# MLP matmuls whose moving columns come from the two halves in turn, with a shorter matmul time in the list scheduler

## Chip, cores and metric

The kernel runs on one core of one Trainium2 chip. The metric is the device time of one execution in microseconds, lower is better.

## What is computed

Random-feature attention over 4 batches, 8 heads, 576 positions (all float32), then two MLPs over its 2304 tokens. The reference, cut:

```python
def _attn_ref(q, k, v, omega):            # (4, 8, 576, 64), omega (128, 64)
    def phi(x):
        h = np.einsum('bhsd,md->bhsm', x, omega) - sum(x * x) / 2
        return np.exp(h - max(h)) / np.sqrt(m)
    q_p, k_p = (phi(q_s), phi(k_s))
    kv = np.einsum('bhsm,bhsd->bhmd', k_p, v)
    return einsum(q_p, kv) / (einsum(q_p, sum(k_p)) + 1e-06)
...
x = attention, as (2304, 512)
h = x @ w_in;  g = h * sigmoid(h);  x = g @ w_out                        # d_ff 2048
g = x @ w_gate;  x = (g * sigmoid(g)) * (x @ w_val) @ w_out2             # d_ff 1536
```

## The kernel before, in words

**Attention** (the first 118 us) works through pairs of heads in steps of 128 positions. Its matmuls (lines 751, 795, 842, and the transposes at 811 and 867) are not touched. Two short bursts of matmuls of a zero tile, 384 columns wide, stand in it: nine at line 734 at the very start, seven at line 903 a little later.

**The MLPs** have four phases in a row: up 1 (`up_phase(0)`, weights `w_in`), down 1 (`down_phase(0)`, `w_out`), up 2 (`w_gate` and `w_val`), down 2 (`w_out2`). The token axis is held in three slices `s` of 2 x 384 columns (`N = 384`, `NSB = 3`), transposed: features on partitions, tokens along the row. Every 2 x 2 block product is done with seven products instead of eight (`PROD`, `ORDER`; operands `A..`/`S..` of the weights, `B..`/`T..` of the activations). Each operand is split into a high part of type float32r and a low part, and a product of two operands is three matmuls: high by high, high by low, low by high. So an up product (`products`, line 1097) is 2 x 3 matmuls, and a down step (line 1472) 2 x 2 x 3; each matmul has 128 x 128 weights and 384 moving columns and adds into one PSUM bank, `ps[b][:, :N]`.

Around the matmuls: ACT copies PSUM banks on (`copy`, lines 1114 and 1413), applies silu (line 1138) and makes high parts (lines 410, 580, 1280, 1331); DVE adds banks (line 1171), makes low parts (lines 423, 591, 1284, 1335) and differences (lines 613, 1355); `conv_job` (lines 322 to 440) loads float64 weights (`L322`), turns them into float32 with ACT (line 343, reads every second word), DVE (lines 350, 357, which reads every second word too) and POOL sums (line 376), and keeps them or stores them to `wd_out` (line 440); line 1123 stores an up phase's result to `g_d`, line 1305 loads it for the down phase.

**The order of the work** on ACT, DVE, POOL and SP is set when the kernel is built, by a list scheduler that runs beside the emission of the matmuls. It keeps a modelled clock per engine (`clk`). After each product, `clk["PE"]` moves on by `6 * MM` (up) or `12 * MM` (down), and `flush` emits all work on the other engines that the model finds ready by then. `MM` is the modelled time of one matmul in us:

```python
    MM = 0.1735
...
            clk["PE"] = t + 6 * MM
...
                    clk["PE"] = t + 12 * MM
```

The engines run their queues in that order, each instruction waiting for what it needs. Nothing on the chip reads `MM`.

Of the kernel before, what the change touches and what calls it, by code (L numbers as in the profile page):

```python
# [42 lines left out]
def kernel(  # L43
# [34 lines left out]
    N = 384  # L78
# [20 lines left out]
    ps = [pp.tile([P, 512], F32, name=f"ps{i}") for i in range(8)]  # L99

    def cut(t, o, n):
        return t[:, o : o + n]

    W_AT, T_AT, X_AT = 0, 7168, 10752
    S_AT, C_AT, R_AT, SUM_AT, XR_AT = 0, 3840, 5376, 7424, 8448
# [126 lines left out]
    def flush(now):  # L232
        while True:
            best = None
            for o in urgent:
                t = o.ready()
                if t is not None and t <= now and (best is None or t < best[0]):
                    best = (t, o)
            if best is None:
                break  # L240
            urgent.remove(best[1])
            best[1].emit()
        while True:

            best = None
            for i, (name, st) in enumerate(streams.items()):
                o = st.best(now + st.ahead, name in ("z", "wd") and clk["dma"] > now + 5.0)
                if o is not None:
                    t = max(o.ready(), clk[o.eng]) + 0.1 * i
                    if best is None or t < best[0]:  # L250
                        best = (t, st, o)
            if best is None:
                break
            best[1].emit(best[2])
# [19 lines left out]
    def need(*keys):  # L274
        for k in keys:
            while k not in T:
                st, o = maker.get(k, (None, None))
                if st is None:
                    u = [o for o in urgent if k in o.outs]
                    if not u:  # L280
                        assert drain(), f"{k} is made nowhere"
                        continue
                    o = u[0]
                need(*o.ins)
                if o.ready() is None:

                    assert drain(), f"{k}: stuck"
                elif k not in T:
                    if st is None:
                        urgent.remove(o)  # L290
                        o.emit()
                    else:
                        while st.q[o.eng][0] is not o:
                            p = st.q[o.eng][0]
                            need(*p.ins)
                            if p.ready() is None:
                                assert drain(), f"{k}: stuck"
                            elif st.q[o.eng][0] is p:
                                st.emit(p)
                        if k not in T and o.ready() is not None:  # L300
                            st.emit(o)

    f_raw = Free("raw", [cut(fa, R_AT + i * 1024, 1024) for i in range(2)])
    f_c = Free("c", [cut(fa, C_AT + i * 512, 512) for i in range(3)])
    f_sum = Free("sum", [cut(fa, SUM_AT, 1024)])
    f_z = Free("z", [])
    f_w = Free("w", [cut(ra, W_AT + i * 1792, 1792) for i in range(6)])
# [748 lines left out]

    later_on.append((1, last_nums))

    MM = 0.1735


    LEND, lent = {(1, 0): ("T3", "T4", "B22",)}, []
# [2 lines left out]
    def up_phase(m, seq, hook):  # L1067
# [17 lines left out]
        def products(n, p, b, start, stop, extra=()):  # L1085
            i, kind, s = seq[n]
            oa, ob = PROD[p]
            need(("W", kind, i), ("X", m, s, ob), *extra)
            wh, wl = (cut(x, OPA[oa] * 256, 256) for x in W[kind, i])
            xh, xl = X[m, s, ob]  # L1090
            t = clk["PE"]
            for k in [("W", kind, i), ("X", m, s, ob), *extra]:
                t = max(t, T[k] + 0.1)
            c = 0
            for j in range(2):
                for l, r in ((wh, xh), (wh, xl), (wl, xh)):
                    nc.tensor.matmul(  # L1097
                        ps[b][:, :N],
                        cut(l, j * P, P),
                        cut(r, j * N, N),  # L1100
                        start=start and c == 0,
                        stop=stop and c == 5,
                        skip_group_check=True,
                    )
                    c += 1
            clk["PE"] = t + 6 * MM
            T[K("P", n, p)] = clk["PE"]
# [79 lines left out]
        for _, n, p in sorted(slots):  # L1187
# [3 lines left out]
            a, b = ps[A[n % 2]], ps[B[n % 2]]  # L1191
            hook(n, p)
            flush(clk["PE"])
            if p == 1:
                products(n, 1, A[n % 2], True, False, [K("h", n - 2, 0)] if n > 1 else [])
                copy(n, 1, b[:, :N], a[:, :N], "AB", free=[("a", n - 2, 3)])
                if m == 0 and n == 0:
                    flush(clk["PE"] + 0.2)
                    later_on.pop(0)[1]()
                    mark(5, 6)  # L1200
            elif p == 6:
                products(n, 6, B[n % 2], False, False, [K("AB", n)])
                copy(n, 6, ps[E][:, :N], b[:, :N], "BE", free=[("a", n - 1, 1)])
            elif p == 5:
# [110 lines left out]
    def down_phase(m, Wd, hook, gap_until=None):  # L1315
# [78 lines left out]
        BANKS = {1: 0, 2: 0, 5: 2, 3: 2, 6: 4, 7: 4, 4: 6}  # L1394
# [55 lines left out]
        for s in range(NSB):  # L1450
            for p in ORDER:
                for k in range(np_):
                    hook(s, p, k)
                    flush(clk["PE"])
                    keys = [K("hi", s, p, k), K("lo", s, p, k)]
                    keys += [("Wd", m, p, g) for g in {2 * k // 3, (2 * k + 1) // 3}]
                    if k == 0 and p in BEFORE:
                        keys += [K("v", s, BEFORE[p], e) for e in range(2)]
                    if k == 0 and p in (1, 5) and s:
                        keys += [K("v", s - 1, {1: "C11", 5: "C12"}[p], e) for e in range(2)]  # L1460
                    need(*keys)
                    t = clk["PE"]
                    for x in keys:
                        t = max(t, T[x] + 0.1)
                    hi, lo = ops.pop((s, p, k))
                    for j in range(2):
                        i = 2 * k + j
                        wh, wl = (cut(t, (i % 3) * 256, 256) for t in Wd[p, i // 3])
                        h, l = cut(hi, j * N, N), cut(lo, j * N, N)
                        for e in range(2):  # L1470
                            for c, (a, b) in enumerate(((wh, h), (wh, l), (wl, h))):
                                nc.tensor.matmul(  # L1472
                                    ps[BANKS[p] + e][:, :N],
                                    cut(a, e * P, P),
                                    b,
                                    start=p in FIRST and i == 0 and c == 0,
                                    stop=p in LAST and i == fp - 1 and c == 2,
                                    skip_group_check=True,
                                )
                    clk["PE"] = t + 12 * MM  # L1480
                    for t in (hi, lo):
                        n = len(lent)
                        lent[:] = [x for x in lent if x is not t]
                        if len(lent) < n:
                            f_op.give(t)
                        elif t is not gap or (s, p) != gap_until and not gone:
                            f_z.give(t)
                        else:
                            gone.append(t)
                    if (s, p, k) == (*(gap_until or (0, 0)), np_ - 1) and not gone:  # L1490
                        f_z.q = deque(x for x in f_z.q if x[0] is not gap)
                        gone.append(gap)
                    if s == NSB - 1 and (k == np_ - 1):
                        for g in range((fp + 2) // 3):
                            for t in Wd.pop((p, g)):
                                f_op.give(t)
                T[K("P", s, p)] = clk["PE"]
                ended(s, p)
# [37 lines left out]
    seq1 = up_order(("in",), FP[0], True, True)  # L1536
    Wd1, wd_ops = down_ops(0)
    d1 = down_phase(0, Wd1, lambda *a: hook_d1(*a), (NSB - 1, 6))

    def z_first(m, *names):  # L1540
# [81 lines left out]
    seq2 = up_order(("gate", "val"), FP[1], False, False)  # L1622
    Wd2, wd_ops2 = down_ops(1)
    d2 = down_phase(1, Wd2, lambda *a: None)

    def hook2(n, p):
# [63 lines left out]
```

## Time and profile before

| | |
|---|---|
| time, median of 3 runs | 884.25 us (883.42 to 886.79) |
| span of the profiled execution (its own time is given by this span alone) | 881.1 us |
| median less span | 3.15 us |
| PE busy | 866.9 us (98%), 6889 matmuls |
| DVE, ACT, POOL busy | 620.3 us (70%), 546.5 us (62%), 165.6 us (19%) |
| attention, up 1, down 1, up 2, down 2 | 0 to 118.2, to 298.5, to 480.7, to 745.6, to 881.1 us |

PE is TensorE's matmul, PEld its weight load, which overlaps matmuls. Matmuls are pipelined: the duration of one (334 ns) is longer than the distance from one start to the next, and the distance is what a stream of them costs. Busy shares are averages; the wait that ends last in a stretch says what more speed there is worth. Times are us from the span's start.

### The profile page before, as it was taken

How to read it: one execution, taken by the hardware profiler on the slowest of the kernel's cores; microseconds unless marked ns; L12 is line 12 of the kernel's file. 1: busy time of each engine (PE TensorE's matmuls, PEld its weight loads, DVE VectorE, ACT ScalarE, POOL GpSimd, SP SyncE). 2: the span in 40 equal slices, each digit the busy share in tenths (PEclk: the TensorE clock that was granted, in tenths of full speed). 3: DMA queues.
4: the chain of work that ended last, by engine and by line, in shares of the span. 5: the costliest groups of instructions: out<-in, count | busy, mean ns of one | idle time of the engine just before them, and what ended most of it. 6: DMA issues, size and time to landing. Idle time of an engine off the chain costs nothing.

```text
span 881.1 us, 18161 instructions
## 1 busy us (share of the span) xinstructions
PE 866.9 (98%) x6889; PEld 843.1 (96%) x6889; DVE 620.3 (70%) x1016; ACT 546.5 (62%) x1166; POOL 165.6 (19%) x204
## 2 busy tenths in 40 slices
PE   9999999999999989999999999999999999999998
PEld 7888899999999989999998999999999999999998
DVE  4888877565634895885899898555555538978773
ACT  6999868666667764454466865454545357655552
POOL 0487830054520000000000044131212100000000
PEclk9999999999999999999999999999999999999999
DMA  8589776389999837338315467352525267573502
GB/s 275 180 288 298 229 254 219 132 274 307 304 294 390 290 136 231 110 92 243 97 60 194 157 210 245 113 200 96 198 96 173 78 234 244 171 248 107 181 1 72
DMA packets 110119, 170.08 MB, mean 193 GB/s; under 512 B 9424, under 2 KB 94032, under 8 KB 110032
## 3 DMA queue, kind: packets, MB, share of 16 engines
q1 hardware_dynamic: 109808, 168.69, 58.7%
q8 instruction: 54, 0.88, 0.4%
q10 hardware_dynamic: 224, 0.23, 0.1%
q14 instruction: 33, 0.27, 0.1%
HBM read 107.02 MB, written 61.87 MB: 192 GB/s over the span
## 4 chain that ended last, share of the span: by engine, by line
PE 73%; issue 7%; DVE 7%; DMA 7%; ACT 4%; POOL 2%; SPq 1%; DVEq 0%; ACTq 0%; POOLq 0%
PE ps L1097 32%; PE ps L1472 31%; PE ps L751 4%; DMA g_d<-fa 2%; PE ps L795 2%; POOL fa L376 2%; PE ps L811 2%; DMA wd_out<-fa 1%; PE ps L842 1%; ACT kq L767 1%; DVE ra L423 1%; DVE fa L357 1%; DMA ra<-g_d 1%; DVE ra L1335 1%; DMA fa<-in_moe_w_out 1%
## 5 line engine op out<-in xcount | busy, mean ns | idle before, releaser
L376 POOL TENSOR_TENSOR fa<-fa 128x256 f32<-128x256 f32 x124 | 105.9, 869 | 526.0 <-DVE fa L357 317.3
L1097 PE MATMUL ps<-ra 128*128 128x384 f32 x840 | 156.0, 335 | 1.6 <-ACT ps L1114 1.5
L1097 PE MATMUL ps<-rc,ra 128*128 128x384 f32 x840 | 154.8, 334 | 0.7 <-ACT ps L1114 0.7
L1097 PE MATMUL ps<-rb,ra 128*128 128x384 f32 x840 | 154.7, 334 | 0.5 <-ACT ps L1114 0.5
L1097 PEld LDWEIGHTS ps<-ra 128*128 128x128 f32 x840 | 146.2, 188 | 2.8 <-ACT ps L1114 2.8
L1097 PEld LDWEIGHTS ps<-rc,ra 128*128 128x128 f32 x840 | 146.2, 188 | 1.7 <-ACT ps L1114 1.7
L1097 PEld LDWEIGHTS ps<-rb,ra 128*128 128x128 f32 x840 | 146.3, 188 | 1.1 <-ACT ps L1114 1.1
L1114 ACT ACTIVATE ps<-ps 128x384 f32<-128x384 f32 x180 | 85.8, 476 | 84.5 <-PE ps L1097 75.5
L1171 DVE TENSOR_TENSOR fa<-fa,ps 128x384 f32<-128x384 f32 x120 | 66.2, 552 | 99.7 <-ACT ps L1114 71.7
L1331 ACT ACTIVATE ra<-fa 128x768 fp32r<-128x768 f32 x86 | 72.6, 846 | 68.7 <-PE ps L1472 49.1
L1335 DVE TENSOR_TENSOR ra<-fa,ra 128x768 fp32r<-128x768 f32 x81 | 77.5, 957 | 30.9 <-PE ps L1472 15.0
L1472 PE MATMUL ps<-ra,rb 128*128 128x384 f32 x516 | 95.7, 335 | 2.3 <-DVE ra L1335 2.3
L1472 PEld LDWEIGHTS ps<-ra,rb 128*128 128x128 f32 x516 | 89.8, 188 | 3.5 <-DVE ra L1335 3.4
L1472 PE MATMUL ps<-ra,rc 128*128 128x384 f32 x482 | 89.3, 335 | 1.9 <-DVE ra L1335 1.9
L1472 PE MATMUL ps<-ra 128*128 128x384 f32 x486 | 86.3, 335 | 1.2 <-ACT ra L1331 0.7
L1472 PEld LDWEIGHTS ps<-ra,rc 128*128 128x128 f32 x482 | 83.8, 188 | 3.3 <-DVE ra L1335 3.1
L1472 PEld LDWEIGHTS ps<-ra 128*128 128x128 f32 x486 | 84.3, 188 | 1.9 <-ACT ra L1331 1.0
L767 ACT ACTIVATE kq<-ps,nb 128x128 f32<-128x128 f32 x288 | 79.8, 411 | 9.2 <-DVE nb L765 8.6
L1355 DVE TENSOR_TENSOR fa<-ra,fa 128x768 f32<-128x768 f32 x63 | 60.1, 954 | 2.4 <-DMA ra<-g_d 1.7
L1138 ACT ACTIVATE fa<-fa 128x384 f32<-128x384 f32 x84 | 43.8, 521 | 27.5 <-DVE fa L1171 27.5
L343 ACT ACTIVATE fa<-fa 128x512 f32<-128x512 f32 x65 | 44.1, 679 | 17.8 <-DMA fa<-in_moe_w_in 6.6
L765 DVE TENSOR_REDUCE nb<-ps 128x4 f32<-128x512 f32 x72 | 48.1, 681 | 6.7 <-PE ps L751 3.1
(112 smaller groups left out, 1120.4 us busy)
## 6 DMA issues: line engine op xcount, KB each, us to landing
g_d<-fa SPq DMA_DIRECT2D x168, 192.0 KB, 3.7
fa<-g_d SPq DMA_DIRECT2D x42, 384.0 KB, 4.7
ra<-g_d SPq DMA_DIRECT2D x42, 384.0 KB, 4.1
fa<-in_moe_w_out SPq DMA_DIRECT2D x28, 512.0 KB, 5.2
fa<-in_moe_w_in SPq DMA_DIRECT2D x16, 512.0 KB, 5.0
wd_out<-fa SPq DMA_DIRECT2D x12, 512.0 KB, 3.3
fa<-in_moe_w_gate SPq DMA_DIRECT2D x12, 512.0 KB, 4.0
fa<-in_moe_w_val SPq DMA_DIRECT2D x12, 512.0 KB, 5.4
```

The source lines that it names most:

```text
L343: nc.scalar.activation(c, word(h, 1).bitcast(F32), AF.Prelu, scale=2.0**-112, alpha=-(2.0**32))
L376: f(blk(f"S{n}"), blk(l), blk(r))
L765: nc.vector.reduce_max(nb, x, axis=AX.X, negate=True)
L767: nc.scalar.activation(e[:, g // 2, g % 2, h * M : (h + 1) * M], x[:, g, :], AF.Exp, bias=nb[:, g : g + 1])
L1097: nc.tensor.matmul(ps[b][:, :N], cut(l, j * P, P), cut(r, j * N, N), start=start and c == 0, stop=stop and c == 5, skip_group_check=True,)
L1114: nc.scalar.activation(out() if callable(out) else out, src, AF.Copy)
L1138: nc.scalar.activation(b["t"], src, AF.Silu)
L1171: nc.vector.tensor_add(t, t if in_place else p5[n], ps[bank_][:, :N])
L1331: nc.scalar.activation(ops[s, p, k][0], src(), AF.Copy)
L1335: nc.vector.tensor_sub(l, src(), h.bitcast(F32))
L1355: (nc.gpsimd if eng == "POOL" else nc.vector).tensor_sub(z(PLACE[to]), z(PLACE.get(l, l)), z(PLACE.get(r, r)))
L1472: nc.tensor.matmul(ps[BANKS[p] + e][:, :N], cut(a, e * P, P), b, start=p in FIRST and i == 0 and c == 0, stop=p in LAST and i == fp - 1 an ...
```

## The change

The moving operand of the MLP matmuls is read in another order: column 0 of the 384, column 192, column 1, column 193, and so on (`halves`). The PSUM side is written as pairs (`woven`), which is the plain order of its addresses: step `b` over pairs, `a` within one. So the addresses written are as before, and what lies in them is the product's columns in woven order. Each of the four phases weaves once more, all other work is per column and doesn't mind, and the host undoes four weavings on the output. Nothing else is changed on the chip but the scheduler's `MM`, from 0.1735 to 0.1640, by which the same instructions on ACT, DVE and SP come in another order.

```diff
+    def halves(t):
+        return t.rearrange("p (a b) -> p b a", a=2)
+
+    def woven(t):
+        return t.rearrange("p (b a) -> p b a", a=2)
...
-    MM = 0.1735
+    MM = 0.1640
...
                 for l, r in ((wh, xh), (wh, xl), (wl, xh)):
                     nc.tensor.matmul(
-                        ps[b][:, :N],
+                        woven(ps[b][:, :N]),
                         cut(l, j * P, P),
-                        cut(r, j * N, N),
+                        halves(cut(r, j * N, N)),
...
                             for c, (a, b) in enumerate(((wh, h), (wh, l), (wl, h))):
                                 nc.tensor.matmul(
-                                    ps[BANKS[p] + e][:, :N],
+                                    woven(ps[BANKS[p] + e][:, :N]),
                                     cut(a, e * P, P),
-                                    b,
+                                    halves(b),
...
-    return np.ascontiguousarray(r.results[0]["out_0"].T)
+    out = r.results[0]["out_0"].reshape(512, 6, 384)
+    for _ in range(4):
+        out = out.reshape(512, 6, 192, 2).swapaxes(2, 3).reshape(512, 6, 384)
+    return np.ascontiguousarray(out.reshape(512, 2304).T)
```

PE's and POOL's queues keep their order; line numbers after the change are 6 higher.

**DVE at the start of down 1.** `ra<-fa,ra` makes the low part of an activation operand for the next products, `fa<-ra,fa` and `fa<-fa` are the differences of operands, `rc<-rc` is the low part of a weight of the later products. Before:

```order
L1335 TENSOR_TENSOR ra<-fa,ra 128x768
L1284 TENSOR_TENSOR rc<-rc 128x512
L1355 TENSOR_TENSOR fa<-ra,fa 128x768
...
L1355 TENSOR_TENSOR fa<-ra,fa 128x768
L1335 TENSOR_TENSOR ra<-fa,ra 128x768
L1284 TENSOR_TENSOR rc<-rc 128x768 x2
L1284 TENSOR_TENSOR rc<-rc 128x512
L1355 TENSOR_TENSOR fa<-ra,fa 128x768
L1335 TENSOR_TENSOR ra<-fa,ra 128x768
L1284 TENSOR_TENSOR rc<-rc 128x768 x2
L1284 TENSOR_TENSOR rc<-rc 128x512
```

Now:

```order
L1361 TENSOR_TENSOR fa<-fa 128x768
L1290 TENSOR_TENSOR rc<-rc 128x512
L1341 TENSOR_TENSOR ra<-fa,ra 128x768
L1290 TENSOR_TENSOR rc<-rc 128x768 x2
L1361 TENSOR_TENSOR fa<-fa 128x768
...
L1361 TENSOR_TENSOR fa<-ra,fa 128x768
L1290 TENSOR_TENSOR rc<-rc 128x512
L1341 TENSOR_TENSOR ra<-fa,ra 128x768
L1290 TENSOR_TENSOR rc<-rc 128x768 x2
L1361 TENSOR_TENSOR fa<-ra,fa 128x768
L1290 TENSOR_TENSOR rc<-rc 128x512
```

The first three weight parts stand earlier, between other operands than before; the blocks of three that stood between two operands are broken up.

**ACT in the middle of up 1**, where weights are converted beside the products. L1114 (now L1120) are the copies of PSUM that the next product waits for, L1138 (L1144) silu, L343 and L410 (L349 and L416) belong to the conversion. Before:

```order
L1114 ACTIVATE ps_81<-ps_79 128x384
L343 ACTIVATE fa<-fa 128x512
L410 ACTIVATE ra<-fa 128x256
L410 ACTIVATE ra<-fa 128x512
L343 ACTIVATE fa<-fa 128x512
L1138 ACTIVATE fa<-ps_84 128x384
L1138 ACTIVATE fa<-fa 128x384
L1114 ACTIVATE ps_83<-ps_81 128x384
```

Now:

```order
L1120 ACTIVATE ps_81<-ps_79 128x384
L349 ACTIVATE fa<-fa 128x512
L1144 ACTIVATE fa<-fa 128x384
L416 ACTIVATE ra<-fa 128x256
L1144 ACTIVATE fa<-ps_84 128x384
L349 ACTIVATE fa<-fa 128x512
L1120 ACTIVATE ps_83<-ps_81 128x384
L416 ACTIVATE ra<-fa 128x512
```

Two silus stand between the two copies as before, but three conversion steps instead of four: the second L410 (L416) has moved behind the second copy.

## Rows read from the trace of the kernel before

**Rows 1.** The page: busy time and share by engine; then the last chain's shares.
```profile
PE 866.9 (98%) x6889; PEld 843.1 (96%) x6889; DVE 620.3 (70%) x1016; ACT 546.5 (62%) x1166; POOL 165.6 (19%) x204
...
PE ps L1097 32%; PE ps L1472 31%; PE ps L751 4%; DMA g_d<-fa 2%; PE ps L795 2%; POOL fa L376 2%; PE ps L811 2%; DMA wd_out<-fa 1%; PE ps L842 1%; ACT kq L767 1%; DVE ra L423 1%; DVE fa L357 1%; DMA ra<-g_d 1%; DVE ra L1335 1%; DMA fa<-in_moe_w_out 1%
```

**Rows 2.** Busy time by phase: stretch, its us, engines, clock, DMA share, GB/s.
```profile
0.00:118.20 118.20, 115.58 (x2548) 98.61 (x2549) 93.51 (x206) 103.30 (x338) 68.71 (x92) 1.00 0.78 247
118.20:298.50 180.30, 179.23 (x1067) 177.22 (x1066) 105.24 (x195) 126.58 (x270) 43.98 (x48) 1.00 0.82 276
298.50:480.70 182.20, 177.38 (x1010) 174.37 (x1009) 148.32 (x183) 99.61 (x149) 0.00 (x0) 1.00 0.49 154
480.70:745.60 264.90, 263.24 (x1515) 262.04 (x1514) 176.69 (x322) 149.37 (x310) 52.95 (x64) 1.00 0.52 170
745.60:881.10 135.50, 131.47 (x757) 130.83 (x755) 96.58 (x115) 67.65 (x100) 0.00 (x0) 1.00 0.41 135
```

**Rows 3.** The last chain in order of time: start, us, what; undisturbed product stretches.
```profile
545.78 199.96 PE ps L1097 x1152
...
763.11 114.54 PE ps L1472 x659
```

**Rows 4.** Busy time of line 1097 alone, then of line 1472 alone, whole span.
```profile
0.00:881.10 881.10, 440.41 (x2520) 436.54 (x2520) 1.00 0.59 193
...
0.00:881.10 881.10, 309.07 (x1764) 305.45 (x1764) 1.00 0.59 193
```

**Rows 5.** Zero-tile bursts on the timeline, then durations (ns min/median/max) of the first.
```profile
1.32 3.25 PE L734 MATMUL ps<-zero 128*128 128x384 f32 x9 [1.32 <-DVE zero L717]
...
7.99 1.51 PE L903 MATMUL ps<-zero 128*128 128x384 f32 x7
...
L734 PE MATMUL ps<-zero x9: 522/522/688, 1.3 to 4.0; 128*128 128x384 f32 x9
```

**Rows 6.** Weight loads of four transposes on the timeline, and durations of all such loads.
```profile
61.80 0.42 PEld L811 LDWEIGHTS ps<-ident,kq 128*128 128x128 f32 x4
...
L811 PEld LDWEIGHTS ps<-ident,kq x144: 137/140/144, 11.5 to 116.6; 128*128 128x128 f32 x144
```

**Rows 7.** Groups by shape (busy us, mean ns): stepped reads, then plain ones, of 512.
```profile
L343 ACT ACTIVATE fa<-fa 128x512 f32<-128x512 f32 x65 | 44.1, 679 | 17.8 <-DMA fa<-in_moe_w_in 6.6 <-DMA fa<-in_moe_w_gate 3.7 <-DMA fa<-in_moe_w_val 3.0
...
L410 ACT ACTIVATE ra<-fa 128x512 fp32r<-128x512 f32 x15 | 9.3, 621 | 1.5 <-POOL fa L376 1.5
```

**Rows 8.** Busy time in three stretches: up 1, down 1's start, down 1 to up 2.
```profile
193.00:253.00 60.00, 58.93 (x333) 57.31 (x332) 34.38 (x66) 38.80 (x85) 28.74 (x32) 1.00 0.95 310
298.00:328.00 30.00, 27.04 (x152) 26.03 (x152) 28.73 (x34) 18.29 (x29) 0.00 (x0) 1.00 0.57 203
...
448.00:538.00 90.00, 86.63 (x487) 83.84 (x486) 83.41 (x150) 62.69 (x128) 15.04 (x16) 1.00 0.54 173
```

**Rows 9.** Busy time in one long stretch of up 2.
```profile
560.00:740.00 180.00, 180.00 (x1040) 180.00 (x1039) 105.68 (x191) 92.44 (x191) 30.97 (x40) 1.00 0.47 159
```

**Rows 10.** Who waited for whom: us in total, times, longest.
```profile
PEld ps L1472 <- DVE ra L1335: 7.3, 9, 2.0
...
PEld ps L1097 <- ACT ps L1114: 5.5, 9, 1.6
```

## The prediction

> **What bounds the kernel now.** First the page: PE is busy 98% of the span, and the chain of work that ended last lies on lines 1097 and 1472, the two lines that change, for 63% of it [rows 1]. A busy share of pipelined matmuls says little alone, so next the busy time by phase [rows 2]: in the four MLP phases PE is idle 1.07, 4.82, 1.66 and 4.03 us. The last 4.03 holds the end of the kernel after the last product, some 3.8 us. So nearly all of the 763 us from 118.2 on is a stream of products with small holes, and what counts is the distance from one product to the next.
>
> That distance is read from undisturbed pieces of the last chain [rows 3]. A piece ends with the whole duration of its last matmul, 0.334 us: (199.96 - 0.33) / 1151 = 0.1734 us in up 2, and (114.54 - 0.33) / 658 = 0.1736 in down 2, which has a few small waits in it. I take **173.4 ns**. The number of products is 2520 + 1764 = **4284** [rows 4]. 4284 x 0.1734 = 743 us, which with the idle time makes up the four phases.
>
> What are 173.4 ns made of? The zero-tile burst at the very start [rows 5] runs at the slower clock, 1.2 GHz, as its distances say (the clock's own records begin later): nine matmuls of the same 128 x 128 by 384 shape span 3.25 us, the last of which lasts 0.52, the first start-to-start being longer by 0.166 (688 against 522). (3.25 - 0.52 - 0.166) / 8 = 0.320 us, 384 columns at 1.2 per ns and nothing on top. At twice that clock the columns alone would take **160.0 ns**. So 13.4 ns per product lie on top of the columns at the full clock, and did not show at the lower one.
>
> I looked for its cause in what the trace allows. The second burst, at line 903, has zeros in both operands and starts a new sum each time: (1.51 - 0.33) / 6 = 0.197 us, with some disturbance in it, so neither data nor adding into PSUM is what costs. The weight load is not the limit either: four loads of 128 x 128 float32 before transposes take 0.42 us with 0.14 for one [rows 6], (0.42 - 0.14) / 3 = 0.093 us apart, far under 173. What is left is the path on which the 384 float32 columns are read at full speed, and the order of that reading is exactly what the change alters. It can alter it in both directions.
>
> **The change, part by part.** *Products.* No row shows a matmul with a stepped moving operand, so this is bounded. From below: the columns alone, 160.0 ns, a saving of 13.4 x 4284 = 57.4 us. From above: a stepped read that costs what it costs the other engines. ACT at line 343 reads every second word of 512 and takes 679 ns, against 621 at line 410 for a plain read of 512 [rows 7]: 58 / 512 = 0.113 ns per element, 43 ns on 384 columns, so 217 ns and 186 us more. The middle end is no change at all. For the value I use the scheduler's constants for their size: the old one, 173.5, is the measured distance (173.4) within 0.1 ns, so the model counts real distances, and the new one, 164.0, is the distance that a working change would have, 4.0 ns above the bare columns. That is 173.5 - 164.0 = 9.5 ns, and 9.5 x 4284 = **40.7 us** less.
>
> The Trainium skill ("TensorE: Matmul & The Clock Gate", Back-to-back issue gap) gives N / 1.2 for a cold matmul and N / 2.4 + 2.5 ns for a warm one; by it a warm product of 384 columns takes 162.5 ns. The first half agrees with the 320 ns here, the second does not with 173.4: this case's products are slower than the page's, so there is something to win. By its figure the saving would be an estimated 10.9 x 4284 = 46.7 us and the result about 845 us.
>
> *What isn't shortened.* Three stretches are nearly filled by something else [rows 8]. From 193 to 253 us the DMA engines are busy 95% of the time at 310 GB/s, with PE idle 1.07 us in holes: weights for the rest of up 1 and for down 1 arrive here. Products that need 5.5% less time (9.5 / 173.4) find no DMA to feed them, so all 60 x 0.055 = 3.3 us are given back. From 298 to 328 DVE is busy 28.73 of 30 us and PE idle 2.96: again all, 1.6 us. From 448 to 538 DVE is busy 83.41 of 90 us and PE idle 3.37; a stretch of 85.1 us would have DVE at 98%, and I give back half, 2.5 of 4.9 us. Together **7.4 us**. Between ends of 0 and 40.7 this is what those rows bear; if all the cover went, rival 2 has the price.
>
> In the rest of the MLPs there is room: from 560 to 740 us PE has no hole, while DVE is busy 105.7 and ACT 92.4 of 180 us and the DMA engines 47% [rows 9]. There the shorter products bring their full 5.5%. Attention, 118.2 us, and the end after the last product stay.
>
> *The scheduler's order.* A shorter MM moves work on ACT, DVE and SP relative to the products; PE's and POOL's queues stay. What PE waits for most is DVE's low parts at line 1335 (7.3 us in 9 waits) and ACT's copies at line 1114 (5.5 in 9) [rows 10]. In DVE's queue at the start of down 1 the blocks of three weight parts that stood between two operands are broken up and the first parts are moved forward; in ACT's queue in up 1 one conversion step leaves the way of a copy. Both suit a faster PE. They cannot return more than those 12.8 us and could add as much where a store or load on SP, itself moved, comes later; I count them as **0**. The stores to `g_d` that SP now issues between other loads are covered by the products until the next down phase, and would cost as holes in PE if that cover went.
>
> *Host side and PSUM.* The addresses written in PSUM are as before, and the un-weaving is on the host: 0.
>
> **Sum.** 881.1 - 40.7 + 7.4 = 847.8 us of span. The median of the runs is 3.15 us above this span; carried over, 847.8 + 3.2 = **851 us**.
>
> **Rivals.** 1. *The columns come from two places in turn and cost more* (slower). Neighbouring columns lie together now; after the change each lies 192 columns from the one before. If such a step costs TensorE anything beyond what it pays now, every one of the 4284 products pays, and no cover hides it, since PE is the bound. It decides from the point at which a product takes over 173.4 ns. By ACT's price it is 186 us, 884 + 186 = 1070 us; if each column took two clocks, 320 ns, it would be 4284 x 146.6 = 628 us and 1512. For it: ACT's row. Against it: 13.4 ns show that reading in address order isn't free either, and the constant of 164. Chance 0.10.
>
> The Trainium skill speaks for this rival ("SBUF — State Buffer", Door 1, in its note on cachelines): lines have 16 bytes, two hits per line are needed for full bandwidth, and each crossing to a new line pays. By that rule float32 columns read in turn from two halves cross at every column. No row here shows TensorE doing so.
>
> 2. *The products get shorter, but DVE, ACT or the DMA take over more widely* (smaller gain). Then only stretches with clear room gain: 118 to 193, 253 to 298 and 553 to 746, 313 us, x 0.055 = 17 us, so 867 us. For it: DVE's share in down 1, 148.3 of 182.2 us [rows 2]. Against it: 180 us without a hole at 59% of DVE. Chance 0.08.
>
> 3. *The reading order doesn't matter* (no change). The 13.4 ns belong to something that the order doesn't touch, such as a fixed pause between products. For it: only the lack of a row on a stepped operand. Against it: it doesn't show at the lower clock. The model then counts PE too fast; the moved work shifts the result by some us either way, 880 to 888, about 884. Chance 0.12.
>
> **How the numbers follow.** Forecast 0.70, rivals 0.10, 0.08 and 0.12. The forecast's own range is 834 (160 ns a product: 57.4 - 7.4 = 50 us less) to 863 (166 ns and twice the give-back). The range over all, **838 to 884**, leaves out rival 1, the upper half of rival 3 and the lowest 4 in 100 of the forecast. A measurement of this kernel tells about 0.5% (4.4 us) from no change. Faster by more than that: 0.70 + 0.08 = 0.78; within it 0.12; slower 0.10.
>
> **What would show it.** Right: undisturbed chain pieces with 162 to 166 ns per product and the same duration less what was saved; PE's idle time in the MLPs up from 11.6 us to 15 to 20, most of it at 190 to 250, around 300 and 430 to 520 us; up 2's long stretch without a hole and shorter by a twentieth. Wrong: a distance of 173 ns (rival 3) or above (rival 1); or a distance of 164 with PE idle for over 25 us (rival 2).

## The result and the profile after

The changed kernel takes **853.2 us** (median of 4 runs, 851.99 to 855.45) against 883.93 us of the kernel before on the same chip (4 runs, 883.42 to 886.79): ratio 0.9651, 95% interval 0.9628 to 0.9673. The forecast was 851, faster. The profiled execution has a span of 851.7 us, 29.4 less than before.

The page, and the busy time by phase (columns as in [rows 2]):

```profile
PE 823.9 (97%) x6889; PEld 796.4 (93%) x6889; DVE 623.8 (73%) x1016; ACT 552.5 (65%) x1166; POOL 164.8 (19%) x204
```

```profile
118.10:293.30 175.20, 169.48 (x1067) 165.99 (x1065) 108.47 (x193) 129.45 (x271) 42.52 (x48) 1.00 0.84 284
293.30:469.20 175.90, 168.61 (x1008) 165.15 (x1009) 147.47 (x180) 99.47 (x150) 0.00 (x0) 0.99 0.51 159
469.20:722.20 253.00, 247.90 (x1514) 245.44 (x1513) 178.15 (x324) 152.31 (x309) 54.11 (x64) 1.00 0.56 178
722.20:851.70 129.50, 124.11 (x758) 122.63 (x756) 97.34 (x116) 68.03 (x101) 0.00 (x0) 1.00 0.43 142
```

DVE and ACT run the same instructions as before, PE is busy 43 us less. But ACT is busy 6.0 us longer and DVE 3.5: the two reads of every second word in `conv_job` alone take 9.9 and 7.6 us more. First DVE's before, then DVE's and ACT's now (ACT's before is in [rows 7], 679 ns):

```profile
L357 DVE SCALAR_TENSOR_TENSOR fa<-fa 128x512 uint32<-128x512 uint32 x65 | 48.4, 745 | 0.5
...
L363 DVE SCALAR_TENSOR_TENSOR fa<-fa 128x512 uint32<-128x512 uint32 x65 | 56.0, 862 | 0.7
...
L349 ACT ACTIVATE fa<-fa 128x512 f32<-128x512 f32 x65 | 54.0, 833 | 20.2 <-DMA fa<-in_moe_w_in 5.7
```

ACT's slower read goes with the woven products, not with the order of the work: it takes 844 ns in the run with woven products and the old order, and 678 ns in the run with plain products and the new order (the first two experiments). In the attention phase, which has no woven product, it is as it was, 742 and 737 ns. ACT's plain read of 512 (line 410, now 416) stays at 621 and 619 ns. How much of what is given back below comes from this was not tested.

The four phases are shorter by 5.1, 6.3, 11.9 and 6.0 us, and PE's idle time in them is 5.72 + 7.29 + 5.10 + 5.39 = 23.5 us, against 11.6 before [rows 2]. The distance from one product to the next comes from undisturbed pieces of the last chain (start, us, what), to be read beside [rows 3]:

```profile
612.92 109.11 PE ps L1103 x670
722.03 7.03 DMA ra<-g_d
...
740.84 96.92 PE ps L1478 x595
```

With 0.326 us for the last matmul of a piece: (109.11 - 0.33) / 669 = 0.1626 and (96.92 - 0.33) / 594 = 0.1626 us, in up and down phases alike. I write **162.5 ns**, the value in the runs of bare products below, and 173.33 for plain reads, from there too. Before it was 173.4.

The account is 4284 x 10.83 ns (173.33 - 162.5) = **46.4 us** won by the products, of which 46.4 - 29.4 = **17.0 us** were given back. Counting the same products in both traces, the give-back lies here (by the old kernel's times): 118 to 193 us 1.6; 193 to 253 2.2; 253 to 298 0.7; **298 to 328 5.7**; 328 to 448 0.1; **448 to 538 3.6**; 538 to 746 1.0; 746 to the end 2.1. The 150 matmuls that took 29.9 us from 298 on now take 33.9, so this place is slower than before.

At the start of down 1, DVE waits for a load from `g_d`, PE for DVE, and then the clock falls. First DVE and PE on the timeline, then three stretches by engine, with the granted clock behind the counts:

```profile
303.12 0.95 DVE L1341 TENSOR_TENSOR ra<-fa,ra 128x768 fp32r<-128x768 f32 x1
306.45 0.96 DVE L1361 TENSOR_TENSOR fa<-ra,fa 128x768 f32<-128x768 f32 x1 [2.37 <-DMA ra<-g_d]
...
304.13 2.22 PE L1478 MATMUL ps<-ra 128*128 128x384 f32 x12 [1.26 <-DVE ra L1341]
308.33 9.89 PE L1478 MATMUL ps<-ra 128*128 128x384 f32 x48 [1.98 <-DVE ra L1341]
```

```profile
293.40:309.70 16.30, 12.29 (x69) 11.15 (x70) 13.65 (x16) 8.79 (x13) 0.00 (x0) 1.00 1.01 336
309.70:313.10 3.40, 3.40 (x13) 3.40 (x12) 3.33 (x5) 2.83 (x4) 0.00 (x0) 0.50 0.34 129
313.10:320.00 6.90, 5.92 (x36) 5.50 (x35) 6.37 (x9) 3.69 (x6) 0.00 (x0) 1.00 0.00 1
```

PE was idle for 4.0 of 16.3 us, then ran at half the clock (1.2 GHz) from 309.7 to 313.1, where ten products cost 320 ns each, 1.6 us more than at 162.5. Before, the clock was full from its first record to the end of the products. A hole also costs more than its idle time: the start after the first product behind it comes at 267 ns instead of 162.5 (the twelve products at 304.13 span 2.22 us, which is 0.267 + 10 x 0.1625 + 0.33). In the kernel before it came at 280 instead of 173. With the slow clock this is a part of why 17.0 us are given back while PE's idle time grew by 11.9.

### The profile page after: what moved, and what is told of

Same layout as the page of the kernel before. It is cut to its first block, busy times and chain, and to the rows that moved or that the text cites. A ratio compares the mean times of both kernels' runs of the same rounds, so it can differ in the third digit from the quotient of the medians.

```text
span 851.7 us, 18196 instructions
## 1 busy us (share of the span) xinstructions
PE 823.9 (97%) x6889; PEld 796.4 (93%) x6889; DVE 623.8 (73%) x1016; ACT 552.5 (65%) x1166; POOL 164.8 (19%) x204
## 4 chain that ended last, share of the span: by engine, by line
PE 76%; DVE 7%; DMA 7%; issue 4%; ACT 3%; POOL 2%; SPq 0%; DVEq 0%; ACTq 0%; POOLq 0%
PE ps L1103 36%; PE ps L1478 29%; PE ps L757 4%; PE ps L801 2%; PE ps L817 2%; DMA wd_out<-fa 2%; PE ps L848 2%; DMA ra<-g_d 2%; POOL fa L382 2%; DVE fa L363 1%; DMA fa<-in_moe_w_val 1%; DVE ra L1341 1%; DMA fa<-in_moe_w_out 1%; DVE ra L429 1%; PE ps L873 1%
## 5 line engine op out<-in xcount | busy, mean ns | idle before, releaser
L1103 PE MATMUL ps<-ra 128*128 128x384 f32 x840 | 148.4, 328 | 6.1 <-ACT ps L1120 4.0
L1103 PE MATMUL ps<-rb,ra 128*128 128x384 f32 x840 | 146.3, 327 | 2.1 <-ACT ps L1120 2.1
L1103 PE MATMUL ps<-rc,ra 128*128 128x384 f32 x840 | 145.8, 326 | 1.5 <-ACT ps L1120 1.5
L1103 PEld LDWEIGHTS ps<-ra 128*128 128x128 f32 x840 | 137.6, 189 | 9.0 <-ACT ps L1120 5.8
L1103 PEld LDWEIGHTS ps<-rb,ra 128*128 128x128 f32 x840 | 137.6, 189 | 3.6 <-ACT ps L1120 3.3
L1103 PEld LDWEIGHTS ps<-rc,ra 128*128 128x128 f32 x840 | 137.8, 189 | 2.5 <-ACT ps L1120 2.4
L1120 ACT ACTIVATE ps<-ps 128x384 f32<-128x384 f32 x180 | 85.4, 477 | 67.7 <-PE ps L1103 63.4
L1341 DVE TENSOR_TENSOR ra<-fa,ra 128x768 fp32r<-128x768 f32 x81 | 77.4, 955 | 21.6 <-PE ps L1478 13.4
L1478 PE MATMUL ps<-ra 128*128 128x384 f32 x486 | 84.0, 332 | 6.8 <-DVE ra L1341 5.7
L1478 PE MATMUL ps<-ra,rb 128*128 128x384 f32 x516 | 89.9, 327 | 0.4 <-DVE ra L1341 0.4
L1478 PEld LDWEIGHTS ps<-ra 128*128 128x128 f32 x486 | 80.7, 192 | 9.0 <-DVE ra L1341 7.4
L1478 PE MATMUL ps<-ra,rc 128*128 128x384 f32 x482 | 83.9, 327 | 2.2 <-DVE ra L1341 2.2
L349 ACT ACTIVATE fa<-fa 128x512 f32<-128x512 f32 x65 | 54.0, 833 | 20.2 <-DMA fa<-in_moe_w_in 5.7
L1144 ACT ACTIVATE fa<-fa 128x384 f32<-128x384 f32 x84 | 43.6, 519 | 25.5 <-DVE fa L1177 25.2
L363 DVE SCALAR_TENSOR_TENSOR fa<-fa 128x512 uint32<-128x512 uint32 x65 | 56.0, 862 | 0.7
```

Source lines behind the costliest of these rows:

```text
L349: nc.scalar.activation(c, word(h, 1).bitcast(F32), AF.Prelu, scale=2.0**-112, alpha=-(2.0**32))
L363: nc.vector.scalar_tensor_tensor(c, word(h, 0), 29, c, op0=ALU.logical_shift_right, op1=ALU.bitwise_or)
L1103: nc.tensor.matmul(woven(ps[b][:, :N]), cut(l, j * P, P), halves(cut(r, j * N, N)), start=start and c == 0, stop=stop and c == 5, skip_gro ...
L1120: nc.scalar.activation(out() if callable(out) else out, src, AF.Copy)
L1144: nc.scalar.activation(b["t"], src, AF.Silu)
L1341: nc.vector.tensor_sub(l, src(), h.bitcast(F32))
```

## The experiments

**The two halves of the change.** One kernel has the woven reads with the old `MM`, the other the plain reads with the new one.

```diff
-    MM = 0.1640
+    MM = 0.1735
```

> Woven reads kept, the scheduler's MM back at 0.1735, so ACT, DVE and SP have the order of the kernel before. Theory 1 (the shorter distance of 162.5 ns is all that counts; the new MM only fits the order to it): undisturbed products 162.5 ns, PE's holes larger than the 29 us of the change, time 853 to 862. Rival (the new order brings part of the gain by itself): over 865. If the order is worth nothing: 851 to 855.

Measured: 854.1 us, ratio 0.9669 (0.9636 to 0.9702), profiled span 850.7. Counted over the same products 16.3 us are given back, not more than with the change, so that part of theory 1 failed.

```diff
-                        woven(ps[b][:, :N]),
+                        ps[b][:, :N],
...
-                        halves(cut(r, j * N, N)),
+                        cut(r, j * N, N),
```

(and the same in the down phase; `MM` stays 0.1640)

> Plain reads, MM 0.1640: the new order alone. Theory 1: products stay at 173.3 ns and the time within 880 to 888, about that of before. Rival (the order brings part of the gain): under 879.

Measured: 885.95 us, ratio 1.0032 (1.0018 to 1.0046). One chain piece shows the distance:

```profile
547.82 199.98 PE ps L1097 x1152
```

(199.98 - 0.33) / 1151 = 0.1735. The new order alone is slower by 0.3%, and with short products it can't be told from the old one. (In the profiled execution the clock fell here too, to 0.50 from 299.0 to 302.4 us.) The whole gain belongs to the reads, as theory 1 had it.

**Which orders of reading are fast.** Three kernels hold nothing but products, 36 per pattern, each pattern on a line of its own. They leave the whole computation out.

```python
far(d, n): columns 0, d, 1, d + 1, ... n - 1, d + n - 1      # halves are far(192)
quarters:  0, 96, 192, 288, 1, 97, ...      every fourth: 0, 4, 8, ..., 1, 5, ...
```

> The computation is left out; 36 products per pattern of the moving operand, all warm. Theory A (two neighbouring columns read one after the other from the same place is what costs 10.8 ns; any order that goes to another place at each column avoids it): halves, quarters, eighths 162.5; every even then every odd column 173 or as halves, every fourth 162.5. Theory B (each crossing to another 16-byte line costs): every fourth column, quarters and eighths over 173.3, halves an exception by two lines kept open. Theory C (the weight load takes turns from a plain read): with 64 of 128 weight columns the plain read costs about 168, with 32 about 165, at 384 columns. Theory D (a fixed pause per product): plain 512 columns 213.3 + 13.3 = 226.7 and 256 columns 120.0; if it is a share of the columns 231.1 and 115.6. Bfloat16 under A or C about 162.5 plain already. Distance between the two places: if a part of the address decides, some of 193 to 256 and 2048 columns fall back to 173.

The timeline of the first of them (start, us, line; the distance is the us less the last matmul's duration, through 35; where the first products of a pattern came at other distances, the steady distance behind them is given). In turn: plain, halves, sixths, quarters, eighths, even then odd columns, every fourth, two columns from each half in turn, four columns from each half in turn:

```profile
25.35 6.40 PE L81 MATMUL ps<-mv,w 128*128 128x384 f32 x36
31.59 6.01 PE L83 MATMUL ps<-mv,w 128*128 128x384 f32 x36
37.43 8.56 PE L85 MATMUL ps<-mv,w 128*128 128x384 f32 x36
45.83 7.56 PE L87 MATMUL ps<-mv,w 128*128 128x384 f32 x36
53.23 12.15 PE L89 MATMUL ps<-mv,w 128*128 128x384 f32 x36
65.20 12.42 PE L91 MATMUL ps<-mv,w 128*128 128x384 f32 x36
77.44 12.66 PE L93 MATMUL ps<-mv,w 128*128 128x384 f32 x36
89.92 9.06 PE L95 MATMUL ps<-mv,w 128*128 128x384 f32 x36
98.81 7.06 PE L97 MATMUL ps<-mv,w 128*128 128x384 f32 x36
```

Distances: plain 173.3, halves **162.5**, sixths 233, quarters 205, eighths 333, even then odd 340, every fourth 347, pairs 247, fours 191 ns. Two places 193, 196, 200, 208, 256 and 2048 columns apart take 162.5 too, 194 apart 163.3. Then plain reads with 32 weight columns, with 512 and 256 moving columns each plain and in halves, and bfloat16 plain and in halves:

```profile
159.25 6.40 PE L117 MATMUL ps<-mv,w 128*32 128x384 f32 x36
165.50 8.33 PE L119 MATMUL ps<-mv,w 128*128 128x512 f32 x36
173.67 7.93 PE L121 MATMUL ps<-mv,w 128*128 128x512 f32 x36
181.44 4.47 PE L123 MATMUL ps<-mv,w 128*128 128x256 f32 x36
185.75 4.18 PE L125 MATMUL ps<-mv,w 128*128 128x256 f32 x36
...
193.74 6.03 PE L129 MATMUL ps<-mb,wb 128*128 128x384 bf16 x36
199.60 13.26 PE L131 MATMUL ps<-mb,wb 128*128 128x384 bf16 x36
```

- Theory C, the weight load, falls: with a quarter of the weight columns the plain read still costs 173.3.
- Theory D holds: 512 plain columns cost 226.7 = 213.3 + 13.3 and 256 cost 119.9 = 106.7 + 13.2, so it is a fixed pause per product. Halves leave 2.5 of it (512: 215.8). At 256 halves give 111.7, and 128 plain columns about the same, 111.5: a bound of another kind.
- Theory A holds only for exactly two places. Quarters, eighths and every fourth should have been 162.5 and are slower than plain.
- Theory B has the sign of quarters, eighths and every fourth, and it made halves an exception, by two lines kept open. Two columns from each half in turn stay in the same two lines and take 247, so that reason fails.
- Bfloat16 has no such pause in a plain read (162.5), and halves cost it 364.

> The computation is left out; 36 products per pattern, the first column of a pair from one place, the second d columns further on (the second place overlaps the first for small d; the numbers don't matter). Theory A (a plain read pays a pause of 10.8 ns once per product, a read that alternates between exactly two places pays none, wherever they are): 162.5 for every d from 8 on; for d of 1 to 4, which stay within one 16-byte line, 162.5 too. Rival (the two places must be in different parts of the memory): small d at 173 or above. Start: halves from column 1 or 4 stay at 162.5, while the plain read from 4 takes 175.6 as in the first series; if lines of 64 bytes decide, plain from 16 and from 384 take 173.3. Plain and halves in turn: a mean of 167.9 if the pause belongs to one product, 162.5 or 173.3 if it belongs to a change of mode. 320 columns: plain 146.7, halves 135.8.

All d of 1, 4, 8, 16, 32, 64, 128 and 192 give 162.5, d = 2 gives 163.3. So the rival is out: the places may overlap. Halves from column 1 take 163.3 and from 4 162.5; plain reads take 173.2 to 175.3 by their start, where no simple rule by lines came out (from 16 173.2, from 384 174.0). Plain and halves in turn: 167.9, so the pause belongs to one product. 320 columns: 146.7 and 135.8, as expected.

> The computation is left out; 36 products per pattern. Is it the two places, or only the form of a pattern whose innermost step counts two columns? Pairs of neighbours turned round (1, 0, 3, 2) read the same lines as a plain read in nearly its order: 162.5 if the form alone decides, 173 or more if the places do. Each column twice from one address: 162.5 by the form. Every other column in pairs: as every fourth before, over 300, if what costs is the step of the outer count; halves of each half in turn: 162.5.

Plain, halves, plain but described and written as pairs, pairs turned round, each column twice, every other column in pairs:

```profile
25.21 6.40 PE L89 MATMUL ps<-mv,w 128*128 128x384 f32 x36
31.45 6.01 PE L91 MATMUL ps<-mv,w 128*128 128x384 f32 x36
37.30 6.44 PE L93 MATMUL ps<-mv,w 128*128 128x384 f32 x36
...
62.30 6.40 PE L101 MATMUL ps<-mv,w 128*128 128x384 f32 x36
68.54 6.01 PE L103 MATMUL ps<-mv,w 128*128 128x384 f32 x36
74.39 12.88 PE L105 MATMUL ps<-mv,w 128*128 128x384 f32 x36
```

173.3, 162.5, 174.5, 173.3, 162.5, 353. The form alone, pairs innermost, doesn't decide: plain pairs and turned pairs pay the pause. The first of these also writes PSUM as pairs, as the changed kernel does, so the write is not what brings the gain. Taken together, the pairs that are fast are those whose two places each move on by **one column** from pair to pair; with two columns from pair to pair (plain in effect, or turned) the pause is there, and with four a product takes more than 320 ns, the time of twice as many columns. Halves of each half in turn, also one column a step, gave 162.5 as expected. Why the chip pauses was not found.

**What gave 17 us back.** First the DMA, where from 190 to 245 us it was busy 93%. This kernel leaves out three quarters of ten loads (two for each of five weight blocks). It and the next one ran once each; the four spans of the changed kernel lie between 850.2 and 853.7 us.

```diff
-                nc.sync.dma_start(out=r.bitcast(U32), in_=wsrc[kind][i, h])
+                z = 256 if kind == "out" and i >= 3 else 1024
+                nc.sync.dma_start(out=r[:, :z].bitcast(U32), in_=wsrc[kind][i, h][:, :z])
```

> As the change, but the last five loads of down weights in up 1 bring a quarter of their bytes (the rest of the buffer holds old data), 3.8 MB less where 16.8 MB move from 190 to 245 us. Theory (the DMA paces this stretch): PE's idle time there falls from 3.1 us to under 1, and DMA's share from 0.93 to about 0.75; the rest is unchanged, span 849. Rival (what PE waits for there is its place in ACT's queue behind conversion steps that wait for DVE or POOL): idle time stays over 2.5 us.

The stretch in the changed kernel, then in this one:

```profile
190.00:245.00 55.00, 51.94 (x311) 50.08 (x311) 36.78 (x63) 37.79 (x80) 27.52 (x32) 1.00 0.93 305
```

```profile
190.00:245.00 55.00, 53.28 (x321) 51.69 (x321) 39.05 (x65) 40.27 (x83) 27.07 (x31) 1.00 0.85 275
```

Idle time falls from 3.06 to 1.72 us, not under 1. Counted over the same products, the give-back from 193 to 253 falls from 2.2 to 0.6 us and before it from 1.6 to 0.1; the span is 847.9, 3.8 less. So loads pace up 1, nearly all of its 3.8 us up to there. The start of down 1 doesn't profit: from 298 to 328 still 5.1 are given back, although the granted clock stayed at 1.00 there. So the fall of the clock is not the main cause of that loss.

Then DVE. The low parts of loaded weights are made for 64 columns only, the rest is left out:

```diff
+            l, h = cut(l, 0, 64), cut(h, 0, 64)
             nc.vector.tensor_sub(l, l.bitcast(F32), h.bitcast(F32))
```

> As the change, but the low parts of weights that are loaded ready (line 1290) are made for 64 columns instead of 448 to 768: DVE loses some 20 us of work around 260 to 320 us, around 455 to 480 and around 700 to 745. Theory (DVE paces the starts of the down phases): PE's idle time from 293 to 320 us falls from 5.3 us to under 3, and from 722 on from 1.9 to under 1. Rival (operands that land late from DRAM pace them): it stays over 4.

The stretch from 293 to 320 in the changed kernel and in this one:

```profile
293.00:320.00 27.00, 21.67 (x114) 20.11 (x115) 23.44 (x28) 15.71 (x24) 0.00 (x0) 0.94 0.67 224
```

```profile
293.00:320.00 27.00, 22.26 (x122) 21.16 (x123) 20.69 (x29) 16.66 (x26) 0.00 (x0) 0.94 0.68 227
```

Idle 5.33 and 4.74: at the start of down 1 idle time stays over 4, as the rival had it, and DVE waits even longer, 3.9 us in one piece, for the load from `g_d`. Yet counted over the same products the give-back from 298 to 328 falls from 5.7 to 3.7, so DVE's work has a part in it. At the start of down 2 it falls from 2.1 us to nothing, as the theory had it; the order of the loads, below, takes away 1.3 of that 2.1 as well. The span is 848.4.

**Casts moved from DVE to ACT.**

```diff
-                elif k in (1, 2):
+                elif k in ():
                     nc.vector.tensor_copy(dst(0, k), src(k))
```

> As the change, with the 30 casts of weight high parts (443 ns each, 13.3 us in all) moved from DVE to ACT. Theory (DVE is what fills the stretch from 440 to 536 us, busy 89.8 of 96): PE's idle time there falls from 7.3 us by 2 to 5, time 848 to 851. Rival (ACT's copies behind more conversion work are later, since ACT at line 1120 is the other thing PE waits for): unchanged or up to 858.

856.12 us, ratio 0.9692 (0.966 to 0.9725). From 440 to 536 us PE's idle time falls from 7.3 to 5.5 us, a little under the theory, but ACT's copies are later elsewhere: PE waits on them in 12 pieces for 10.0 us in all, against 11 for 7.5, and from 118 to 253 the give-back grows from 3.8 to 10.1. (The profiled execution, 859.95 us, is the longest of the four.)

**Loads in the order in which they are needed.** The timeline of down 1's start points at a cause that is no engine's load: the changed kernel asks for block B21 ahead of B22, and the third product needs B22, the fourth B21.

```diff
-    streams["z"].extend(z_first(0, "B21", "B22"))
+    streams["z"].extend(z_first(0, "B22", "B21"))
```

(and the same for the second MLP)

> As the change, but the operand blocks that a down phase loads last come in the order in which they are needed: B22 (third product) ahead of B21 (fourth). Theory (a part of what was given back at the start of down 1 and down 2 is that B22's loads stand behind B21's, so DVE waits for a load and PE for DVE; the hole of 2.3 us at 306 us, and with it the fall of the clock after it): the hole of 2.3 us shrinks to under 1 and the clock stays up, PE's idle time from 293 to 320 us falls from 5.3 to under 3.5, from 722 on from 1.9 to under 1; span 848 to 850.5. Rival (the loads can't start before the last weights of up 1 are free, whatever their order): the hole moves to the fourth product, span 851 to 853.

**849.24 us** (848.78 to 850.73), ratio 0.9612 (0.9596 to 0.9629), span 847.0; the best kernel of this study. The same places in it:

```profile
293.73 9.75 PE L1478 MATMUL ps<-ra 128*128 128x384 f32 x48 [0.56 <-DVE ra L1341]
304.10 10.02 PE L1478 MATMUL ps<-ra 128*128 128x384 f32 x60 [0.62 <-DVE ra L1341]
```

```profile
293.00:320.00 27.00, 24.19 (x133) 23.14 (x133) 26.15 (x31) 16.28 (x25) 0.00 (x0) 0.94 0.65 218
```

The hole of 2.3 us is gone and DVE no longer waits for a load there (ACT still does, 2.6 us in three pieces, for weights from `wd_out`); idle time is 2.8 us, and DVE is now busy 26.15 of 27 us. The give-back from 298 to 328 falls from 5.7 to 3.1, at the end from 2.1 to 0.8. The clock still falls once, from 294.4 to 297.8, after the hole at the very start of the phase, so that part of the expectation failed.

> The same with MM 0.1635. If the two are independent, the sum of their parts: 0 to 3 us under the change.

849.95 us, ratio 0.9616 (0.9601 to 0.9632). `MM` 0.1635 without the other edit, for which I had written

> As the change with MM 0.1635, nearer to the 162.5 ns that a product takes. If the order is worth little: 851 to 855; if the model's distance from the truth costs: under 851.

gave 852.81, ratio 0.9656 (0.9639 to 0.9672). In both pairs `MM` makes no difference that can be told.

> B22 first, and in up 2 the conversion of weights is emitted at most 0.4 us ahead of the model's PE instead of 0.8, so that fewer conversion steps stand before the copies that PE waits for. Theory (the holes from 500 to 535 us are copies behind conversion steps): PE's idle time from 440 to 536 us falls from 7.3 to under 6. Rival (they are weights that are converted late, at a pace that DVE sets): it grows.

851.16 us, ratio 0.9631 (0.9615 to 0.9647). Idle time from 440 to 536 us is 7.4 us, as it was, and counted over the same products the give-back from 448 to 538 grows from 3.6 to 5.2: the theory falls. What paces that stretch is shown only in part, by the casts on ACT.

## Why the prediction was right, and where it was off

- *What bounds the kernel.* Right: with plain reads the time is 886 us, with woven reads 853 to 854, in either order of the work.
- *Where the 13.4 ns are.* Right that it is not the weight load and that the order in which the columns are read decides. My picture of it as a matter of reading at full speed was loose: it is one pause per product, whatever the number of columns. Why the chip pauses stays open.
- *Products: 40.7 us.* Mis-sized: the step that read the new constant as the new distance. It is 162.5, not 164.0 ns, 46.4 us. The scheduler's constant isn't a measurement, and that it came so near is luck. The Trainium skill's formula ("TensorE: Matmul & The Clock Gate", Back-to-back issue gap) gives 162.5 for 384 columns, and the halves agree to the digit; the plain float32r read doesn't.
- *Not shortened: 7.4 us.* Mis-sized, 17.0. For 193 to 253 I had 3.3, it was 2.2, and the DMA is shown to pace it. For 448 to 538 2.5 against 3.6. For 298 to 328 I had 1.6 on the step that a DVE-filled stretch keeps its length; it grew by 4.1 us. The step looked at how busy DVE was and not at what it waited for. Three runs each take away a part of the 5.7 us: loads in the order of need (3.1 left), less work for DVE (3.7) and the old order of the work (3.6). And 5.5 us lie in the other places, where I had put nothing, 1.6 of them from 118 to 193, which the run with less DMA takes away, and 2.1 at the start of down 2.
- *ACT and DVE at their old pace.* A term that I left out without a reason: their reads of every second word became slower, ACT's from 679 to 833 ns.
- *Order: 0.* Right in sum, 0.3% against it with long products, but as two effects that cancel, and that is luck. Against the run with the old order, the new one gives back less from 118 to 253 (3.8 us against 6.7) and more at the starts of the two down phases (7.8 against 4.4). So not all of the moves suit a faster PE, as I had judged from ACT's and DVE's queues; which move costs what is not shown.
- The two errors are of opposite sign, 5.7 and 9.6 us, so the forecast span of 847.8 missed 851.7 by only 3.9. A third one is smaller: I added 3.15 us from span to median, where it was 1.5. Each single execution on record, of either kernel, takes about 1.8 us more than its span; the rest of the 3.15 came from a profiled execution that was faster than the median. That 851 is so close to 853.2 is luck.
- *Sums and signs.* 743 us of products and 11.6 of idle time are 754, not the 763 us of the four phases; I passed over the 8.5 that are missing, of which the late starts behind holes are a part. After the last product 3.5 us remain, not 3.8. At 166 ns and twice the give-back the forecast's own range ends at 867, not at 863. Of the signs, the distance (162.6) and up 2's long stretch without a hole came as said; PE's idle time, 23.5 us, lies above the 15 to 20 that I had named.
- *Rival 1* would have been right for quarters (205), eighths or steps of two (340): at 340 it is 4284 x 166.7 ns, 714 us more. Its rule in the Trainium skill ("SBUF — State Buffer", Door 1, note on cachelines) fits quarters and eighths in direction; it fails for two places in turn and for steps of two columns, which still take two columns from each line. *Rival 2* had a point in that the give-back was more than twice my 7.4, yet far from its 24. *Rival 3* named a fixed pause between products, and that is what it is; it was wrong that the reading order doesn't touch it.

## What to carry to other kernels

Measure the distance between matmul starts and compare it with the columns over the clock; a difference that doesn't depend on the number of columns is a pause per product, and the order in which the moving operand is read may remove it. For float32r on this chip that order is two places in turn, each moving on by one column, which costs a permutation undone once at the end; for bfloat16 it does harm. When the bound engine gets faster, look again at the order of loads at each change of phase: a swap of two names here gave 0.4% more.

## What was unexpected of the hardware

- 384 float32r columns read from two places in turn cost 162.5 ns a product, in address order 173.3; from four places 205, from eight 333. The two places may be the same address.
- The same halves cost bfloat16 364 ns, against 162.5 in address order.
- With 128 float32r weight columns no steady distance was under 111.5 ns: 128 columns, plain or in halves, and 256 columns in halves all stop at 111.5 to 111.7.
- While products are read from two places in turn, ACT's read of every second word takes 821 to 844 ns, by the run, instead of 679; ACT's plain read keeps about 620. Whether it is the order of the products' reads or their faster pace is not shown.
